# Turning the state read's exponentials on VectorE and moving the blocks by transfers inside the chip, in seven of eight batches

## The chip, the cores and the metric

The kernel runs on one core of one Trainium2 chip. A core has a matrix engine (TensorE, PE in the profile; PEld is its loading of weights, which overlaps the matrix work), VectorE (DVE), ScalarE (ACT), GpSimd (POOL), and SyncE (SP), which here only starts transfers. They run their own instruction streams and wait for each other by semaphores. SBUF is the memory on the chip that all of them use, PSUM the small memory into which TensorE writes its results.

The metric is the device time of one execution in microseconds (us). Before the change it is 656.82 us, the median of 3 runs (656.65 to 656.95).

## The reference

Two stages follow each other. The first is an attention between `x` (8 batches, 8 heads, 512 rows, 64 values) and a small `state` (32 rows per head), in both directions:

```python
scores  = scale * np.matmul(x, state.transpose(0, 1, 3, 2))    # softmax over 32 -> a
xread   = np.matmul(a, state)
scores2 = scale * np.matmul(state, x.transpose(0, 1, 3, 2))    # softmax over 512 -> a2
sread   = np.matmul(a2, x)
attn    = np.concatenate([xread, sread], axis=2)
```

The second is a feed-forward block over all 8 x (512 + 32) = 4608 tokens of 512 values, with a hidden width of 2048: `h = tokens @ w_in`, `g = h * tanh(softplus(h))` (called mish), and `g @ w_out`. The change is in `sread`, the state's read of `x`.

## The kernel before, in words

**The tiling.** Each matrix product in the feed-forward block is made of three products of a high and a low part (names ending in `h` and `l`), so each 128x512 piece of output costs three times the passes. For each batch the hidden width is walked in 8 slots (`SLOTS`) of 256. In a slot, `gemm1` multiplies the normalised attention (`ah`, `al`) with the state times `w_in` (`swh`, `swl`) into two PSUM banks `ph`; ScalarE applies mish and writes one tile `g`; VectorE makes its high part `gh` and its low part `gl`; and `gemm2`, two slots later (`LAG`), multiplies these with `w_out` (`wo`) into four PSUM banks `acc`. There is a single `g` tile, so mish of a slot waits until `gl` of the slot before has read it, and there are two `ph` banks, so `gemm1` of a slot waits until mish of the slot before has read them.

**The attention of the next batch** runs beside this. In the loop at the end of the kernel, `key` is the batch whose feed-forward slots run, and `own` is the attention of batch `key + 1`, `prev` that of batch `key`. In slot 3 (slot 4 where `key` is 1), `scores` writes the scaled scores `scs` (128 partitions: 4 head pairs x 32 state rows; two halves `kc` of 512 columns), `soft2` makes the exponentials `e2` of the state read with their sums, and `soft1` those of the other direction, which are then turned by VectorE (`at`) and split into `ah` and `al`. The state read, `sread`, is done a batch later, in slot 3 or 4 of its own batch (for batch 7 in slot 7 of batch 6).

**The step that changes.** `sread` needs `e2` with the 512 positions on the partitions. `e2_transposed` (L376) does that: for each half `kc`, four TensorE transposes of 128x128 into a PSUM bank `e2p`, then one copy by ScalarE to `e2T` in SBUF. For batches 2 to 7 it runs in slot 6 of the batch before (L865), for batch 1 in slot 2 of its own (L859), for batch 0 among the steps of the long string.

**What sets the order.** Up to the end of that string every engine issues in the written order (`InOrder`). From there on only TensorE does (`dve.on = act.on = False`); VectorE, ScalarE and the transfers are ordered by a scheduler before the kernel runs, under the written dependences. Nearly all transfers are issued by SyncE on one queue, in order, and each also waits until the one eight places ahead has landed. That queue carries the loads of `x` in two layouts (`x`, and `xq` in 32x32 blocks: 32 transfers of 32 KB per batch, in pieces of 128 bytes), the state (`sn`), and the stores of results, whose staging tiles `o` are three.

Instructions are all recorded at one helper line, L70, so this text goes by tile names.

Of the kernel before, what the change touches and what calls it, by code (L numbers as in the profile page):

```python
# [9 lines left out]
F32 = mybir.dt.float32  # L10
# [7 lines left out]
P = 128  # L18
B, H, S, NS, D = 8, 8, 512, 32, 64
DM, DF = 512, 2048  # L20
T = S + NS
NC = H // 2
NT = S // P
# [25 lines left out]
def quad(q):  # L49
    return slice(q * NS, (q + 1) * NS)  # L50
# [27 lines left out]
def state_attention_mish_kernel(ctx, tc, x, state, w_in, w_out, out):  # L78

    nc = tc.nc  # L80
    pe, dve, act, pool_e = (InOrder(tc, e) for e in (nc.tensor, nc.vector, nc.scalar, nc.gpsimd))
# [3 lines left out]
    pool = ctx.enter_context(tc.tile_pool(name="pool", bufs=2))  # L85
# [4 lines left out]
    def misc(name):  # L90
        return ps_m.tile([P, 512], F32, tag="m", name=name)
# [117 lines left out]
    def load_state(b):  # L209


        sn = pool.tile([P, H, 32], F32, tag="sn", name=f"sn_{b}", bufs=1)
        if b == 0:
            for g in range(2):
                nc.scalar.dma_start(
                    sn[:, 2 * g:2 * g + 2].rearrange("p h d -> p (h d)"),
                    state[b, 4 * g:4 * g + 4].rearrange("h n d -> (h n) d"))
            return sn
        if b == 1:
            sq[b] = pool.tile([P, H, D], F32, tag="e2T", name=f"sq_{b}")  # L220
            for q in range(4):
                nc.sync.dma_start(sq[b][quad(q)], state[b].rearrange("h n d -> n h d"))
        for q in range(4):
            nc.sync.dma_start(
                sn[q * 32:(q + 1) * 32], state[b].rearrange("h n d -> n h d")[:, :, q % 2 * 32:(q % 2 + 1) * 32])
        return sn
# [39 lines left out]
    @contextmanager  # L266
    def behind(*marks):

        with ExitStack() as st:
            for m in marks:  # L270
                st.enter_context(tc.issue_after(last[m].ins if hasattr(last[m], "ins") else last[m]))
            yield

    bds, bqs, sq = {}, {}, {}
# [8 lines left out]
    def attention(b, sn, xq=None):  # L283
        sc, e2T, srd, aT = {}, {}, {}, {}
# [70 lines left out]
        rs2, e2s = {}, {}  # L355
# [7 lines left out]
        def soft2_e(kc):  # L363
# [9 lines left out]
            dve.reciprocal(rs2[kc], sm)  # L373
            e2s[kc] = e2

        def e2_transposed(kc):  # L376
            e2 = e2s[kc]
            pt = misc(f"e2p_{b}_{kc}")
            for t in range(NT):
                pe.transpose(pt[:, t * P:(t + 1) * P], e2[:, t * P:(t + 1) * P], ident)  # L380
            yield
            e2T[kc] = pool.tile([P, NT, P], F32, tag="e2T", name=f"e2T_{b}_{kc}")
            act.copy(e2T[kc].rearrange("p t n -> p (t n)"), pt)


# [125 lines left out]
                soft2_m(kc)  # L511
                whole(soft2_e(kc))

        own.update(soft1=soft1, soft2=soft2)
        return own


# [108 lines left out]
    def gemm2(key, fcs, gh, gl, ntok, ts=None):  # L626

        if key not in accs:
            new_accs(key, ntok)
        for t in ts or range(ntok):  # L630

            for i, fc in enumerate(fcs):
                col = (i * ntok + t) * P
                sl = slice(col, col + P)
                ops = [(gh, 1), (gh, 0), (gl, 1)]
                for n, (g, w) in enumerate(ops):
                    last["PE"] = pe.matmul(
                        accs[key][t], g[:, sl], wo[fc // 2][:, fc % 2, w],
                        start=(fc == 0 and n == 0), stop=(fc == NFC - 1 and n == 2))
            if (key, fcs[-1], t) == (B - 1, NFC - 1, ntok - 1):  # L640
                for part in (slice(0, 256), slice(256, 512)):
                    o = pool.tile([P, 256], F32, tag="e2T", name=f"o_{key}_{t}_{part.start}")
                    act.copy(o, accs[key][t][:, part])
                    (nc.scalar if part.start else nc.sync).dma_start(
                        out[key * T:key * T + S, part].rearrange("(p t) e -> p t e", t=NT)[:, t, :], o)
            elif fcs[-1] == NFC - 1:
                o = pool.tile([P, DM], F32, tag="o", name=f"o_{key}_{t}", bufs=3)
                if t % 2 == 0:
                    dve.tensor_copy(o, accs[key][t])
                else:  # L650
                    act.copy(o, accs[key][t])
                if key == "s":
                    for b4 in range(4):
                        r0 = (4 * t + b4) * T + S
                        nc.sync.dma_start(out[r0:r0 + NS, :], o[b4 * NS:(b4 + 1) * NS, :])
                else:
                    to = out[key * T:key * T + S, :]

                    pieces = [(to.rearrange("(p t) e -> p t e", t=NT)[:, t], o)]
                    if key < 2:  # L660
                        to = to[t * P:(t + 1) * P].rearrange("(p i) e -> i p e", i=NT)
                        pieces = [(to[i], o[quad(i)]) for i in range(NT)]
                    for to, part in pieces:
                        last["store"] = nc.sync.dma_start(to, part)
# [117 lines left out]
    for step in """  # L782
# [13 lines left out]
        what, i = re.fullmatch(r"([a-zA-Z]+)(\d*)", step).groups()  # L796
# [20 lines left out]
    own = at1  # L817
    srds[0] = pool.tile([P, B - 1, 2, D], F32, tag="wt", name="srds", bufs=1)
    for key, j in slots:
        if key == "s":  # L820
            if j == 0:
                second((0, 1), True)
                sreads_transposed()
                second((2, 3))
            g = gemm1_s(j)
            pending.append((key, range(4 * j, 4 * j + 4), g, 2))
            if j:
                second()
            continue
        g = split_g(f"{key}_{j}", mish(key, j, gemm1(key, j, aTs[key], sw)))  # L830
        pending.append((key, (2 * j, 2 * j + 1), g, NT))

        slow = key == 1 and j < 2
        ready = slow or len(pending) > LAG
        n = pending[0][3] // 2
        if ready and not slow:
            second(range(n), True)
        if j == 0:
            prev = own
            if key + 1 < B:  # L840
                own = attention(key + 1, sn_next, xqs.pop(key + 1))
                aTs[key + 1] = own["aT"]
        more = key + 1 < B
        if key == 1 and j == 0:
            prev["soft2"]()


        beside = []
        if key == 1 and j == 1:
            beside += [sw_slice(key, 2)]  # L850
        if j == (3 if key == 1 else 1):
            beside += [sw_slice(key, 6, bank=first_bank), sw_slice(key, 4)]
        if more and j == 7:
            if 1 < key < B - 2:
                beside += [sw_slice(key + 1, 2, bank=first_bank)]
            beside += [sw_slice(key + 1, 0)]
        if key in (2, B - 1) and j == 0:
            beside += [sw_slice(key, 2)]
        if key == 1 and j == 2:  # L859
            beside += [prev["et"](k) for k in range(2)]  # L860
        if more and j == (4 if key == 1 else 3):
            beside += [own["sc"](0)]
        if j == (4 if key == 1 else 3) and key < B - 1:
            beside += [prev["sr"](k) for k in range(2)]
        if more and j == 6:  # L865
            beside += [own["et"](k) for k in range(2)]
        if key == B - 2 and j == 7:
            beside += [own["sr"](k) for k in range(2)]
        together(*beside)
        if more and j == 1:  # L870
            with behind("swl"):
                own["st"](0)
        if ready:
            second((2 * j, 2 * j + 1), j == 0) if slow else second(range(n, 2 * n))
        if more and j in (0, 2):
            with behind("swl"):
                own["x"](j)
                own["x"](j + 1)
        if more and j == (4 if key == 1 else 3):
            own["soft2"]()  # L880
        if more and j == (5 if key == 1 else 3):
            with behind("swh", "swl"):
                own["soft1"]()
        if key + 2 < B and 2 <= j < 6:

            if j == 2:
                xqs[key + 2] = new_xq(key + 2)
            with behind("store"):
                load_xq(key + 2, xqs[key + 2], range((j - 2) * H, (j - 1) * H))
        if key == 1 and j == 3:  # L890
            with behind("store"):
                xss[2] = load_x(2)
        if 1 < key < B - 1 and j == 4:
            with behind("mish"):
                xss[key + 1] = load_x(key + 1)
        if j == SLOTS - 1 and key + 2 < B:
            with behind("mish"):
                sn_next = load_state(key + 2)
# [26 lines left out]
```

## Time and profile before

| | |
|---|---|
| median of 3 runs | 656.82 us (656.65 to 656.95) |
| the profiled execution | 656.5 us, of which the span of recorded instructions is 654.7 us |
| TensorE busy | 647.8 us, 99% of the span, 4742 matrix instructions |
| VectorE busy | 341.1 us, 52% |
| ScalarE busy | 256.9 us, 39% |
| transfers | 82146 packets, 42.35 MB; the main queue takes 22.2% of the 16 transfer engines' span |

The profile is of one execution. A row of its lists names an engine, an operation and the tiles as out<-in; "x64" is a count. In a list in order of time the first column is the start and the second the length, both in us; a bracket at the end gives the idle time before the instruction and what ended it. The chain of waits is followed backwards from the last instruction, so that what it names is what set the end.

### The profile page before, as it was taken

To read this page: it belongs to the slowest core of one execution; us is meant where nothing else is said; L and a number is where in the kernel's file an instruction comes from. 1 tells how busy PE (TensorE), PEld (TensorE's weight loads), DVE (VectorE), ACT (ScalarE), POOL (GpSimd) and SP (SyncE) were. 2 spreads that over 40 slices of the span, in tenths; PEclk is the share of its full clock that TensorE was granted. 3 is DMA by queue.
4 is the path that set the end of the run, shared out by engine and by line. 5 is a ranking of instruction groups with operands and counts; after the bars stand their busy time and mean duration, and the time that the engine had idled before them with its cause. 6 is when DMAs were issued, how large, how long until landed. Compare 5 with 4: busy or idle time off the path is not lost.

```text
span 654.7 us, 11255 instructions
## 1 busy us (share of the span) xinstructions
PE 647.8 (99%) x4742; PEld 519.8 (79%) x4742; DVE 341.1 (52%) x531; ACT 256.9 (39%) x415; POOL 0.7 (0%) x6
## 2 busy tenths in 40 slices
PE   8999999999999999999999999999999999999997
PEld 6677777787778877787778887787778899878886
DVE  5999984283538245554437255544537345232222
ACT  4988943354225322542235223532235334131110
POOL 0000000000000000000000000000000000000000
PEclk9999999999999999999999999999999999999999
DMA  8986213320134003400133003400110001000001
GB/s 325 410 277 195 45 19 76 51 69 1 31 71 102 1 1 87 106 9 1 38 76 90 1 0 93 105 6 2 65 57 9 2 1 65 2 9 25 0 1 64
DMA packets 82146, 42.35 MB, mean 65 GB/s; under 512 B 63280, under 2 KB 71728, under 8 KB 82096
## 3 DMA queue, kind: packets, MB, share of 16 engines
q1 hardware_dynamic: 81664, 41.44, 22.2%
q8 instruction: 37, 0.61, 0.4%
q10 hardware_dynamic: 432, 0.20, 0.1%
q14 instruction: 13, 0.11, 0.0%
HBM read 32.70 MB, written 8.91 MB: 64 GB/s over the span
## 4 chain that ended last, share of the span: by engine, by line
PE 96%; ACT 2%; DMA 1%; SPq 0%; DVE 0%; issue 0%
PE acc L70 54%; PE ph L70 26%; PE swp L70 5%; PE ph_s L70 4%; PE acc_s L70 3%; PE srp L70 1%; PE sc L70 1%; PE e2p L70 1%; DMA wir<-in_moe_w_in_dram 1%; ACT wir L70 1%; PE scT L70 0%; SPq L128 0%; ACT L70 0%; ACT wor L70 0%; ACT swh L70 0%; ACT ah L70 0%
## 5 line engine op out<-in xcount | busy, mean ns | idle before, releaser
L70 PE MATMUL acc<-wo,gh 128*128 128x512 f32 x1024 | 319.9, 394 | 0.0
L70 PEld LDWEIGHTS acc<-wo,gh 128*128 128x128 f32 x1024 | 189.4, 188 | 46.5 <-issue 7.6
L70 PE MATMUL acc<-wo,gl 128*128 128x512 f32 x512 | 199.5, 390 | 0.0
L70 ACT ACTIVATE g<-ph 128x512 f32<-128x512 f32 x128 | 72.4, 597 | 196.6 <-DVE gl L70 166.9
L70 PEld LDWEIGHTS acc<-wo,gl 128*128 128x128 f32 x512 | 96.1, 188 | 20.5
L70 DVE CAST gh<-g 128x1024 fp32r<-128x1024 f32 (+1 forms) x61 | 41.1, 673 | 111.4 <-PE acc L70 108.6
L70 DVE TENSOR_TENSOR gl<-g,gh 128x1024 fp32r<-128x1024 f32 (+1 forms) x65 | 78.4, 1206 | 4.8 <-DVE gh L70 0.5
L70 PE MATMUL ph<-ah,swh 128*128 128x512 f32 x256 | 79.4, 392 | 0.1
L70 PE MATMUL ph<-al,swh 128*128 128x512 f32 x256 | 78.8, 390 | 0.0
L70 PE MATMUL ph<-ah,swl 128*128 128x512 f32 x256 | 78.7, 389 | 0.0
L70 DVE TENSOR_TENSOR swl<-swp,swh 128x512 fp32r<-128x512 f32 (+1 forms) x72 | 41.1, 625 | 65.0 <-ACT swh L70 65.0
L70 PEld LDWEIGHTS ph<-ah,swh 128*128 128x128 f32 x256 | 47.5, 188 | 11.3 <-ACT g L70 0.8
L70 PEld LDWEIGHTS ph<-al,swh 128*128 128x128 f32 x256 | 48.0, 188 | 10.4 <-DVE al L70 0.4
L70 PEld LDWEIGHTS ph<-ah,swl 128*128 128x128 f32 x256 | 48.1, 188 | 10.0
L70 ACT ACT_TABLE_LOAD x35 | 44.9, 1283 | 16.9 <-DVE gl L70 16.1
L70 ACT CAST swh<-swp 128x512 fp32r<-128x512 f32 (+1 forms) x72 | 34.2, 550 | 36.1 <-PE swp L70 36.1
L70 PE MATMUL swp<-w_in_sb,bd 64*32 64x256 f32 x1024 | 33.8, 381 | 0.0
L70 DVE TENSOR_REDUCE nm<-scs 128x1 f32<-128x512 f32 x16 | 10.3, 678 | 34.7 <-ACT scs L70 34.7
L70 PEld LDWEIGHTS swp<-w_in_sb,bd 64*32 64x32 f32 x1024 | 17.4, 106 | 12.7 <-issue 7.8
L70 ACT COPY o<-acc 128x512 f32<-128x512 f32 (+1 forms) x17 | 9.4, 561 | 41.7 <-PE acc L70 39.4
L70 DVE STREAM_TRANSPOSE xT<-xq 128x512 f32<-128x512 f32 x24 | 23.9, 1065 | 3.1 <-PE e2p L70 3.1
L70 DVE COPY o<-acc 128x512 f32<-128x512 f32 x16 | 10.9, 684 | 19.9 <-PE acc L70 19.9
(89 smaller groups left out, 479.1 us busy)
## 6 DMA issues: line engine op xcount, KB each, us to landing
x<-in_x_dram SPq DMA_DIRECT2D x32, 256.0 KB, 3.6
wir<-in_moe_w_in_dram SPq DMA_DIRECT2D x16, 512.0 KB, 10.0
wor<-in_moe_w_out_dram SPq DMA_DIRECT2D x16, 512.0 KB, 7.3
xq<-in_x_dram SPq DMA_DIRECT2D x192, 32.0 KB, 2.3
out_dram<-o SPq DMA_DIRECT2D x23, 256.0 KB, 2.4
out_dram<-o SPq DMA_DIRECT2D x32, 64.0 KB, 1.7
sn<-in_state_dram SPq DMA_DIRECT2D x28, 32.0 KB, 2.2
out_dram<-o_s SPq DMA_DIRECT2D x8, 64.0 KB, 1.7
```

Of the source, the lines that this page charges most:

```text
L70: made = method(*args, **kwargs)
```

## The change

For batches 1 to 7 the eight TensorE transposes and the two ScalarE copies go. In their place `e2_turned` lets VectorE turn each 128x512 half of `e2` in 32x32 blocks into a tile `u`. That leaves each block turned, but in the quarter of 32 partitions where it was. Sixteen transfers from SBUF to SBUF then take block columns from quarter `c` to quarter `q` of `e2T`; each moves 32 partitions x 8 pieces of 32 values (128 bytes), 32 KB in all. `u` has one buffer, which it shares with the scores `scs` (tag `sc`). `e2T` becomes one tile for both halves, with one buffer. The turn comes in slot 4 of the batch before (slot 6 where that is batch 1), and for batch 1 in slot 1 of its own. Batch 0 keeps its transposes. Two small tiles, `sq_1` and the last `o`, move to other tags.

```diff
         if b == 1:
-            sq[b] = pool.tile([P, H, D], F32, tag="e2T", name=f"sq_{b}")
+            sq[b] = pool.tile([P, H, D], F32, tag="o", name=f"sq_{b}", bufs=3)
...
+        def e2_turned():
+
+            both = pool.tile([P, 2 * NT, P], F32, tag="e2T", name=f"e2T_{b}", bufs=1)
+            for kc in range(2):
+                e2T[kc] = both[:, kc * NT:(kc + 1) * NT]
+            u = pool.tile([P, 2, S], F32, tag="sc", name=f"u_{b}", bufs=1)
+            for kc in range(2):
+                dve.transpose(u[:, kc], e2s[kc])
+            v = u.rearrange("i k (t q n) -> i q (k t) n", t=NT, q=4)
+            for c in range(NC):
+                for q in range(4):
+                    nc.sync.dma_start(both[quad(q), :, quad(c)], v[quad(c), q])
+
         def e2_transposed(kc):
...
-            e2T[kc] = pool.tile([P, NT, P], F32, tag="e2T", name=f"e2T_{b}_{kc}")
+            if not e2T:
+                both = pool.tile([P, 2 * NT, P], F32, tag="e2T", name=f"e2T_{b}", bufs=1)
+                e2T.update({k: both[:, k * NT:(k + 1) * NT] for k in range(2)})
...
-        if key == 1 and j == 2:
-            beside += [prev["et"](k) for k in range(2)]
+        if key == 1 and j == 1:
+            with behind("mish"):
+                prev["turn"]()
...
-        if more and j == 6:
-            beside += [own["et"](k) for k in range(2)]
...
+        if more and j == (6 if key == 1 else 4):
+            with behind("mish"):
+                own["turn"]()
```

The scheduler's order changes with it. Three places matter for the prediction. In the rows, numbers behind tile names tell buffers apart and differ between the two kernels; an `e_1` read for `u` is the exponential `e2` of batch 1.

VectorE in the first slots of batch 1, before (`at`, `al` are the turned and the low parts of batch 1's attention, `wo` and `w` the last `w_out` pieces, `swl` the low part for the first slot):

```order
L70 STREAM_TRANSPOSE at_1_1047<-e_1_1_907 128x512
L70 TENSOR_SCALAR sm_0_1161<-sm_0_1161 128x1
L70 TENSOR_SCALAR sm_1_1169<-sm_1_1169 128x1
L70 TENSOR_TENSOR wo_1045<-w_996,wo_1045 128x2x512
L70 RECIPROCAL rs_0_1164<-sm_0_1161 128x1
L70 RECIPROCAL rs_1_1172<-sm_1_1169 128x1
L70 TENSOR_TENSOR al_1050<-at_1_1047,ah_1049 128x512
L70 SCALAR_TENSOR_TENSOR w_1068<-wor_153 128x1024
```

and with the change:

```order
L70 STREAM_TRANSPOSE at_1_1046<-e_1_1_906 128x512
L70 TENSOR_SCALAR sm_0_1160<-sm_0_1160 128x1
L70 TENSOR_SCALAR sm_1_1168<-sm_1_1168 128x1
L70 STREAM_TRANSPOSE u_1223<-e_1_0_1159 128x512
L70 STREAM_TRANSPOSE u_1223<-e_1_1_1167 128x512
L70 TENSOR_TENSOR wo_1044<-w_995,wo_1044 128x2x512
L70 RECIPROCAL rs_0_1163<-sm_0_1160 128x1
L70 RECIPROCAL rs_1_1171<-sm_1_1168 128x1
L70 TENSOR_TENSOR al_1049<-at_1_1046,ah_1048 128x512
L70 SCALAR_TENSOR_TENSOR w_1067<-wor_153 128x1024
```

The two turns stand ahead of the low part of `wo`; everything behind them, up to and past `swl`, keeps its order.

VectorE in the slots where batch 4's softmaxes run (beside batch 3), from the second sum on, before:

```order
L70 TENSOR_REDUCE s_4_1_2825<-e_4_1_2823 128x16
L70 TENSOR_TENSOR e_4_0_2816<-e_4_0_2816,r_4_0_2819 128x512
L70 TENSOR_SCALAR s_4_1_2825<-s_4_1_2825 128x16
L70 STREAM_TRANSPOSE at_0_2840<-e_4_0_2816 128x512
L70 RECIPROCAL r_4_1_2826<-s_4_1_2825 128x16
L70 CAST gh_4_2875<-g_4_2872 128x1024
L70 TENSOR_TENSOR e_4_1_2823<-e_4_1_2823,r_4_1_2826 128x512
L70 TENSOR_TENSOR al_2843<-at_0_2840,ah_2842 128x512
L70 TENSOR_TENSOR gl_4_2876<-g_4_2872,gh_4_2875 128x1024
```

and with the change:

```order
L70 TENSOR_REDUCE s_4_1_2842<-e_4_1_2840 128x16
L70 TENSOR_TENSOR e_4_0_2833<-e_4_0_2833,r_4_0_2836 128x512
L70 TENSOR_SCALAR s_4_1_2842<-s_4_1_2842 128x16
L70 CAST gh_4_2892<-g_4_2889 128x1024
L70 STREAM_TRANSPOSE at_0_2857<-e_4_0_2833 128x512
L70 RECIPROCAL r_4_1_2843<-s_4_1_2842 128x16
L70 TENSOR_TENSOR gl_4_2893<-g_4_2889,gh_4_2892 128x1024
L70 TENSOR_TENSOR e_4_1_2840<-e_4_1_2840,r_4_1_2843 128x512
L70 TENSOR_TENSOR al_2860<-at_0_2857,ah_2859 128x512
```

The two turns of this batch stand some rows ahead of these (behind the reciprocals `rs`), and `gl_4` now comes ahead of two 128x512 operations that it followed. Batches 2, 3, 5, 6 and 7 show the same two moves.

SyncE's queue around batch 1's transfers, before:

```order
L224 DMA sn_1131<-in_state_dram 32x8x32 x4
L141 DMA xq_1098<-in_x_dram 32x8x32 x32
L664 DMA out_dram<-o_0_1180 32x512 x4
L664 DMA out_dram<-o_1_1192 32x512 x4
L224 DMA sn_1795<-in_state_dram 32x8x32 x3
```

and with the change:

```order
L224 DMA sn_1130<-in_state_dram 32x8x32 x4
L141 DMA xq_1097<-in_x_dram 32x8x32 x32
L387 DMA e2T_1222<-u_1223 32x8x32 x16
L680 DMA out_dram<-o_0_1179 32x512 x4
L680 DMA out_dram<-o_1_1191 32x512 x4
L224 DMA sn_1806<-in_state_dram 32x8x32 x3
```

The sixteen moves stand between the load of batch 2's `xq` and the stores of batch 0's first results. On TensorE the only rows that differ are the missing `e2p` rows of batches 1 to 7.

More of the change, by code (lines that the diff above doesn't have):

```diff
@@ L512, in soft2 @@
                 whole(soft2_e(kc))
-        own.update(soft1=soft1, soft2=soft2)
+        own.update(soft1=soft1, soft2=soft2, turn=e2_turned)
         return own
@@ L640, in gemm2 @@
             if (key, fcs[-1], t) == (B - 1, NFC - 1, ntok - 1):
+                last_o = pool.tile([P, DM], F32, tag="e2T", name=f"o_{key}_{t}", bufs=1)
                 for part in (slice(0, 256), slice(256, 512)):
-                    o = pool.tile([P, 256], F32, tag="e2T", name=f"o_{key}_{t}_{part.start}")
+                    o = last_o[:, part]
                     act.copy(o, accs[key][t][:, part])
```

## Prediction

> **What bounds the kernel now.** I read the page's busy times first, then the chain of waits, then the rows of the step that goes.
>
> ```profile
> span 654.7 us, 11255 instructions
> PE 647.8 (99%) x4742; PEld 519.8 (79%) x4742; DVE 341.1 (52%) x531; ACT 256.9 (39%) x415; POOL 0.7 (0%) x6
> PE 96%; ACT 2%; DMA 1%; SPq 0%; DVE 0%; issue 0%
> ```
>
> TensorE works for 99% of the span and makes up 96% of the chain. So TensorE time taken away is gained one to one, if what replaces it makes TensorE wait nowhere. The step that goes lies on that chain; these are the first, the third and the last of seven pieces (start, length, what), the third with the groups around it, from the chain in order of time.
>
> ```profile
> 109.24 0.88 PE e2p L70 x8
> ...
> 217.58 2.72 PE acc L70 x12
> 220.30 0.87 PE e2p L70 x8
> 221.18 2.74 PE acc L70 x12
> ...
> 511.34 0.87 PE e2p L70 x8
> ```
>
> Eight transposes hold the chain for 0.87 us, and the group of twelve products behind them takes 2.74 us where the one ahead of them took 2.72. I count 0.89 us a batch.
>
> **What is removed.** Seven batches x 0.89 us = **-6.2 us** on TensorE, and TensorE's row order differs in nothing else. ScalarE loses 14 copies, 591 ns each in the groups by shape; it is busy 39% and none of these copies is on the chain, so I count nothing.
>
> ```profile
> L70 ACT COPY e2T<-e2p 128x512 f32<-128x512 f32 x16 | 8.7, 591 | 14.8 <-PE e2p L70 12.4 <-PE srp L70 2.3
> L70 DVE STREAM_TRANSPOSE at<-e 128x512 f32<-128x512 f32 x14 | 9.9, 708 | 0.0
> L70 DVE STREAM_TRANSPOSE xT<-xq 128x512 f32<-128x512 f32 x24 | 23.9, 1065 | 3.1 <-PE e2p L70 3.1
> ```
>
> **What VectorE gets.** Two turns of 128x512 a batch. A plain one (`at`) takes 708 ns, one through a strided view (`xT`) 1065 ns. Source and target of `u` are plain rows of 512, so I take the first. Two such in a row occupy 1.22 us of the queue: the pair below starts at 270.11 and the next instruction at 271.33. Two `xT` would occupy about 1.9.
>
> ```profile
> 270.11 1.29 DVE L70 STREAM_TRANSPOSE e<-scs 128x512 f32<-128x512 f32 x2
> 271.33 0.19 DVE L70 TENSOR_SCALAR sm<-sm 128x1 f32<-128x1 f32 x2
> ```
>
> Whether that costs anything depends on who waits behind it; there are two kinds of places.
>
> **Batch 1** is the tight one. The pair goes in ahead of the row at 83.87, in a stretch where VectorE has no idle time at all until 95.05 (only that row has a bracket).
>
> ```profile
> 83.78 0.17 DVE L70 TENSOR_SCALAR sm<-sm 128x1 f32<-128x1 f32 x2
> 83.87 1.22 DVE L70 TENSOR_TENSOR wo<-w,wo 128x1024 fp32r<-128x1024 f32 x1
> ...
> 90.47 1.28 DVE L70 TENSOR_TENSOR swl<-swp,swh 128x512 fp32r<-128x512 f32 x2
> 91.66 1.99 DVE L70 STREAM_TRANSPOSE xT<-xq 128x512 f32<-128x512 f32 x2
> 95.05 0.69 DVE L70 CAST gh<-g 128x1024 fp32r<-128x1024 f32 x1 [1.40 <-ACT g L70]
> ```
>
> So `swl`, which ended at 91.75, now ends at 92.97. TensorE loads it as weights for the first slot of batch 1:
>
> ```profile
> 92.19 0.41 PEld L70 LDWEIGHTS ph<-ah,swl 128*128 128x128 f32 x2
> 86.06 0.62 PE L70 MATMUL acc<-wo,gh 128*128 128x512 f32 x2
> ```
>
> The second of these loads began at 92.41 (0.19 before its end at 92.60). Between VectorE and its waiter lie about 0.09 us (the `gl` that ends at 284.65 and the table load at 284.74, quoted below). 92.97 + 0.09 - 92.41 = **+0.65 us** of TensorE waiting. The low part of `wo` at 83.87 is late too: it now ends at 86.31, and the second product at 86.06, which begins about 86.29, needs it. That is some 0.1 us, and lies inside the 0.65, because VectorE sets the later time on its own. What comes next recovers: `gh` at 95.05 had 1.40 us of idle time ahead of it, more than the 1.22. Bounds: 0 if the pair is hidden by something I don't see, and 1.33 with turns as slow as `xT`'s.
>
> **Batches 2 to 7.** Here the pair goes in at 273.35 (batch 4, the others alike), and the chain to watch is `gl`, then ScalarE's table load, then mish `g`, then the next `gemm1`, which needs the PSUM bank.
>
> ```profile
> 273.22 0.21 DVE L70 RECIPROCAL rs<-sm 128x1 f32<-128x1 f32 x2
> 273.35 0.67 DVE L70 TENSOR_TENSOR e<-e,mx 128x512 f32<-128x512 f32 x1
> 279.59 0.69 DVE L70 TENSOR_REDUCE s<-e 128x16 f32<-128x512 f32 x1 [2.74 <-ACT e L70]
> 282.23 0.68 DVE L70 TENSOR_TENSOR e<-e,r 128x512 f32<-128x512 f32 x1
> 282.82 0.68 DVE L70 TENSOR_TENSOR al<-at,ah 128x512 fp32r<-128x512 f32 x1
> 283.43 1.22 DVE L70 TENSOR_TENSOR gl<-g,gh 128x1024 fp32r<-128x1024 f32 x1
> 284.74 1.28 ACT L70 ACT_TABLE_LOAD   x1 [2.46 <-DVE gl L70]
> 286.04 1.09 ACT L70 ACTIVATE g<-ph 128x512 f32<-128x512 f32 x2
> 287.23 0.41 PEld L70 LDWEIGHTS ph<-ah,swh 128*128 128x128 f32 x2
> ```
>
> The first half of `g` is done at 286.04 + 0.54 = 286.58, and the load that needs its bank begins at 287.23: 0.56 us to spare after 0.09 for the wait. The softmax chain shifts by 1.22, so the sum at 279.59 goes to 280.81. But the new order puts `gl` ahead of the two operations at 282.23 and 282.82, which occupied 1.20 us. So `gl` starts at 283.43 + 1.22 - 1.20 = 283.45. I count **nothing**: the cover is that 0.56 us, and without the changed order each of the six batches would lose 1.22 - 0.56 = 0.66. The two operations that now follow `gl` make `ah` and `al` for a batch that begins three slots later.
>
> **What the queue gets.** Sixteen transfers a batch. The nearest rows are the `xq` transfers: same 32 KB, same 128-byte pieces, but from memory outside the chip.
>
> ```profile
> L141 SPq DMA_DIRECT2D xq<-in_x_dram x192: 560/607/1822, 60.2 to 424.9; - x192
> DMA to landing us min/median/max: 2.0/2.3/4.6
> 60.21 23.21 SPq L141 DMA_DIRECT2D xq<-in_x_dram  x32
> 96.50 3.65 SPq L664 DMA_DIRECT2D out_dram<-o  x8
> 129.62 1.03 PE srp L70 x64
> 521.41 1.03 PE srp L70 x64
> ```
>
> At 23.21 / 32 = 0.73 us each, 16 take 11.6 us of the queue. For batch 1 they run from about 85.2 to 96.8 and have landed by 99.1; the read `srp` is at 129.62. Behind them wait the stores that issued at 96.50 and now come some 0.3 us later. The shortest way is batch 7's: `u` is made at about 493, the moves are down by 507, and the read is at 521.41. All hidden, **0 us**. While `xq` ran, TensorE was as busy as ever, so I expect no contention either.
>
> **What the wait costs TensorE.** The first four `srp` matmuls of a batch waited on 5 semaphores in all; in the listing of the new order they wait on 18, since eight transfer counters are involved.
>
> ```profile
> PEld swp L70 <- issue: 7.8, 22, 0.4
> PEld srp L70 <- issue: 3.0, 8, 0.4
> ```
>
> The start of such a group costs 7.8 / 22 = 0.355 us for `swp` and 3.0 / 8 = 0.375 for `srp`: 0.02 more, which I put to the 5 semaphores. Thirteen more are 0.05 a batch, **+0.35 us** for seven (0 at least; with 0.4, the longest of each row, in place of 0.375 it would be 0.045 x 13 / 5 x 7 = 0.8).
>
> **The sum.** -6.2 + 0.65 + 0.35 = -5.2. The span becomes 649.5, the profiled execution (656.5 before, 1.8 around its span) 651.3. The median of the runs lay 0.3 above that execution, so the forecast is 656.82 - 5.2 = **651.6 us**. The bounds give 650.6 (nothing lost) to 652.7 (1.33 and 0.8 lost).
>
> **Rivals.**
>
> *Nothing is lost:* TensorE's removal is all there is, 656.82 - 6.2 = 650.6. For it: the lost pieces are small. Against: the batch 1 stretch is full.
>
> *The turns are as slow as `xT`'s:* +1.33 at batch 1, and 1.9 - 1.20 - 0.56 = 0.14 in six batches, so 656.82 - 6.2 + 1.33 + 0.35 + 0.84 = 653.1. Against: the plain shapes of the turn.
>
> *VectorE's extra work lands on the path in every batch:* the shift is not taken up by the order, 0.66 x 6 = 4.0 more, 655.6; with slow turns (1.9 - 0.56) x 6 = 8.0 and 1.33, so 660.3. Against: 2.74 us of idle time at 279.59 is of waits, not of work, and `gl` does move ahead. The Trainium skill ("VectorE: DVE Perf Modes", Rules for kernel authors) says to transpose 128x128 on TensorE where PSUM may be the target; by that rule this rival would hold. The trace agrees that TensorE is quicker (0.89 us against 1.22 and the moves), but the rule weighs one operation alone, and here TensorE is the busy engine.
>
> *The moves are slow and hold up the queue (slower):* in batch 1 the stores of batch 0 stand behind them. The fourth result waits for the first store's tile, and TensorE for that result's bank.
>
> ```profile
> 103.83 0.59 ACT L70 COPY o<-acc 128x512 f32<-128x512 f32 x1 [1.82 <-PE acc L70]
> 111.32 0.62 PE L70 MATMUL acc<-wo,gh 128*128 128x512 f32 x2
> ```
>
> That bank is written at 111.32 at the latest, so the copy must start by 110.5, and the first four stores (1.8 us to issue, 1.7 to land) by 107.0: 16 moves may take 107.0 - 85.2 = 21.8 us, 1.36 each. From there every 0.1 us more costs 1.6. At 2.3 us each, if each waited for its landing, the loss is 15 us: 666.6. For it: a single `xq` took 1.82. Against: the median is 0.61, eight are in flight, and nothing here leaves the chip. The Trainium skill ("DMA: Bandwidth & Descriptors", Specifications) asks for at least 512 bytes a piece; the same page ("Why small descriptors are slow (HBM only)") excepts moves inside the chip. No run so far shows which holds.
>
> That the change doesn't do what it says I leave out: the order shows the `e2p` rows gone.
>
> **How the numbers follow.** Forecast 58%, nothing lost 15%, slow turns 13%, every batch 7%, slow moves 7%. Range 650.3 to 654.5: it holds the first three with 0.3 below and over 1 us above, and leaves out the last two. About 0.2% (1.3 us) is what a measurement of this kernel can tell from no change. Faster takes the first three, 86%; 655.6 is within 0.2%, so same gets 5%; the rest, 9%, is slower.
>
> **What would show it.** `e2p` x8 left, with batch 0 alone; `u<-e` near 0.7 us; a wait of PEld for `swl` or its `ph` of 0.5 to 0.8 us near 92 and no wait for `g` in later batches; `e2T` moves issued at about 0.7 us and landed before 100 in batch 1; `srp` groups starting at most 0.1 us later than before. A row of PEld waiting for `ACT g` six times, or stores of batch 0 after 100, would make me wrong.

## The result, and the profile after

The changed kernel takes 651.69 us, the median of 6 runs (651.05 to 651.87), against 656.74 us (656.59 to 657.6) for the kernel before on the same chip: a ratio of 0.992, 95% interval 0.9907 to 0.9932. The forecast was 651.6. The profiled execution took 651.86 us, its span 650.1. Which terms of the sum made that up is another matter, and two of them were wrong.

First the page of the changed kernel (span, busy times, chain of waits by engine).

```profile
span 650.1 us, 11350 instructions
PE 642.0 (99%) x4686; PEld 514.0 (79%) x4686; DVE 348.6 (54%) x545; ACT 249.5 (38%) x401; POOL 0.7 (0%) x6
PE 96%; DMA 2%; ACT 1%; DVE 0%; issue 0%; SPq 0%
```

TensorE has 56 instructions less and 5.8 us less of busy time; it is still the chain. VectorE has 14 more, 7.5 us. Next, the rows of the tiles `e2p` and `u`: the transposes that are left (durations in ns: least, median, most; then the first and last start), the moves and the turns.

```profile
L70 PE MATMUL e2p<-ident,e x8: 270/272/273, 41.9 to 45.4; 128*128 128x128 f32 x8
...
L387 SPq DMA_DIRECT2D e2T<-u x112: 586/609/1532, 85.6 to 499.5; - x112
L70 DVE STREAM_TRANSPOSE u<-e x14: 669/683/701, 84.3 to 488.4; 128x512 f32<-128x512 f32 x14
DMA to landing us min/median/max: 1.9/1.9/4.0
```

Batch 0's eight transposes are left. A turn takes 683 ns, the plain kind. A move takes 609 ns to issue, just as a load of `xq` did, and lands 1.9 us later, where `xq` took 2.3.

The tight place, batch 1, in order of time:

```profile
84.29 1.29 DVE L70 STREAM_TRANSPOSE u<-e 128x512 f32<-128x512 f32 x2
85.51 1.18 DVE L70 TENSOR_TENSOR wo<-w,wo 128x1024 fp32r<-128x1024 f32 x1
85.61 11.01 SPq L387 DMA_DIRECT2D e2T<-u  x16
86.75 0.19 PEld L70 LDWEIGHTS acc<-wo,gh 128*128 128x128 f32 x1 [0.24 <-DVE wo L70]
92.07 1.28 DVE L70 TENSOR_TENSOR swl<-swp,swh 128x512 fp32r<-128x512 f32 x2
92.81 0.19 PEld L70 LDWEIGHTS ph<-ah,swl 128*128 128x128 f32 x1
93.01 0.89 PE L70 MATMUL ph<-ah,swl 128*128 128x512 f32 x2
93.40 0.19 PEld L70 LDWEIGHTS ph<-ah,swl 128*128 128x128 f32 x1 [0.41 <-DVE swl L70]
95.96 0.69 DVE L70 CAST gh<-g 128x1024 fp32r<-128x1024 f32 x1 [0.69 <-ACT g L70]
97.40 3.65 SPq L680 DMA_DIRECT2D out_dram<-o  x8
```

The turns hold VectorE from 84.29 to 85.51, 1.22 us, and TensorE's loading waits twice: 0.24 us for `wo`, 0.41 us for `swl`. The pair of matmuls around the second wait takes 0.89 us, where such a pair takes 0.62. At `gh` the delay is gone: VectorE idles again, for 0.69 us. The last move is issued by 96.62, and the stores that stand behind the moves start at 97.40, so the moves didn't hold them up.

In batch 4, as in the other five, no weight load waits for `g` that didn't before:

```profile
271.87 1.28 DVE L70 STREAM_TRANSPOSE u<-e 128x512 f32<-128x512 f32 x2
...
279.30 0.69 DVE L70 TENSOR_REDUCE s<-e 128x16 f32<-128x512 f32 x1 [2.74 <-ACT e L70]
...
281.94 1.16 DVE L70 TENSOR_TENSOR gl<-g,gh 128x1024 fp32r<-128x1024 f32 x1
...
284.50 1.09 ACT L70 ACTIVATE g<-ph 128x512 f32<-128x512 f32 x2
...
285.87 0.41 PEld L70 LDWEIGHTS ph<-ah,swh 128*128 128x128 f32 x2
```

The sum at 279.30 keeps its 2.74 us of idle time ahead. The first half of `g` is done at 284.50 + 0.54 = 285.04, 0.83 before the load at 285.87 (before: 0.65, with the 0.09 of the wait still to come off both). The cover grew.

And the state read of batch 1. Its first matmul starts at the same time in both profiles, which makes them easy to compare; before, then after:

```profile
129.55 0.94 PEld L70 LDWEIGHTS srp<-x,e2T 128*32 128x32 f32 x64 [0.41 <-issue]
...
130.58 0.73 PE L70 MATMUL acc<-wo,gh 128*128 128x512 f32 x2
```

```profile
129.56 1.14 PEld L70 LDWEIGHTS srp<-x,e2T 128*32 128x32 f32 x64 [0.41 <-issue]
...
130.79 0.74 PE L70 MATMUL acc<-wo,gh 128*128 128x512 f32 x2
```

The idle time ahead of the group is the same 0.41 us. The group itself takes 0.20 us longer, 1.14 against 0.94 for the same 64 loads. This loss shows in no bracket and no list of waits; in the lists of the profile only the group's length and the start of the next group tell of it.

So I took the starts of all 182 groups of TensorE's work behind the long string of batch 0, in the profile of before and in each other profile, and noted where the distance between the two changes. It changes in four kinds of places, and this is the sum for the changed kernel, in us:

| place | change |
|---|---|
| up to 67 us (start-up and batch 0, where nothing is altered) | +0.48 |
| batch 1, at `wo` (0.12) and `swl` (0.30) | +0.42 |
| the seven places where `e2p` stood, 0.89 or 0.90 each | -6.27 |
| the seven state reads | +0.81 |
| end of TensorE's last group | -4.56 |

Without the first row, which turns out not to belong to the change (below), that is -5.04, against -5.05 between the medians.

### The profile page after: what moved, and what is told of

Read it like the earlier page. It is cut to its first block, busy times and chain, and to the rows that moved or that the text cites. A ratio compares the mean times of both kernels' runs of the same rounds, so it can differ in the third digit from the quotient of the medians.

```text
span 650.1 us, 11350 instructions
## 1 busy us (share of the span) xinstructions
PE 642.0 (99%) x4686; PEld 514.0 (79%) x4686; DVE 348.6 (54%) x545; ACT 249.5 (38%) x401; POOL 0.7 (0%) x6
## 4 chain that ended last, share of the span: by engine, by line
PE 96%; DMA 2%; ACT 1%; DVE 0%; issue 0%; SPq 0%
PE acc L70 55%; PE ph L70 27%; PE swp L70 5%; PE ph_s L70 4%; PE acc_s L70 3%; DMA wor<-in_moe_w_out_dram 1%; PE srp L70 1%; PE sc L70 1%; DMA x<-in_x_dram 0%; DVE s L70 0%; DVE e L70 0%; ACT L70 0%; ACT wor L70 0%; ACT ah L70 0%; ACT wir L70 0%; PE srTp L70 0%
```

## The experiments

After each run stands what it told; the table at the end has all of them in the form just shown.

**Is it batch 1's place that costs, and nothing else of VectorE's work?** The first kernel gives batch 1 its TensorE transposes back:

```diff
-        if key == 1 and j == 1:
-            with behind("mish"):
-                prev["turn"]()
+        if key == 1 and j == 2:
+            beside += [prev["et"](k) for k in range(2)]
```

> Batch 1 keeps its eight TensorE transposes in slot 2; batches 2 to 7 are turned by VectorE and moved as in the change. Theory: the 0.42 us that TensorE loses in batch 1 (0.12 waiting for wo, 0.30 for swl) comes from the two turns in VectorE's full stretch, so no wait for wo or swl near 86 to 93 us is left, the 0.20 us at batch 1's state read goes too, and 0.89 us of transposes comes back: 0.3 us slower than the change, about 652.0. Rival (the waits come from the later start of this execution, which lay 0.46 us behind at 63 us): both waits stay, 0.9 us slower.

651.98 us (651.6 to 652.18), ratio 0.9925 [0.991, 0.994]. Neither wait of batch 1 is there, the read of batch 1 loses nothing, six removals stay. Against the changed kernel this loses the 0.89 of batch 1 and wins 0.42 there and about 0.2 at the read: the turn of batch 1 was worth its stall.

The second keeps the turn but lets the scheduler put it behind `swl`:

```diff
-            with behind("mish"):
+            with behind("mish", "swl"):
                 prev["turn"]()
```

> As the change, but batch 1's two turns wait for the low part swl of the first slot, so that on VectorE they come behind swl and xT. Theory: the 0.42 us of waiting for wo and swl is gone and nothing replaces it, since 1.40 us of VectorE's idle time followed there before the change: 0.4 us faster than the change, 651.3. Its moves start about 8 us later and share the queue with the stores of batch 0. Rival (VectorE's work counts wherever it stands): the wait reappears at the next gemm1 or at mish of slot 2, time as the change's 651.7.

651.09 us (650.51 to 651.2), ratio 0.991 [0.9895, 0.9925]. The rows of its batch 1:

```profile
93.29 1.26 DVE L70 STREAM_TRANSPOSE u<-e 128x512 f32<-128x512 f32 x2
94.58 2.60 SPq L387 DMA_DIRECT2D e2T<-u  x4
94.89 0.69 DVE L70 CAST gh<-g 128x1024 fp32r<-128x1024 f32 x1 [0.34 <-ACT g L70]
97.27 3.84 SPq L680 DMA_DIRECT2D out_dram<-o  x8
101.15 7.78 SPq L387 DMA_DIRECT2D e2T<-u  x12
```

The turn now stands in the idle time ahead of `gh`, of which 0.34 us is left, and no load waits for `wo` or `swl`. The moves are partly behind the stores and still long done by 129. The 0.42 us is a price of the place.

**Does the amount of VectorE's work count in batches 2 to 7?** Each pair of turns is done twice:

```diff
-            for kc in range(2):
+            for kc in (0, 1, 0, 1):
                 dve.transpose(u[:, kc], e2s[kc])
```

> The changed kernel, with each batch's pair of turns done twice on VectorE (the second pair writes the same values over the first); moves and read as they are. Theory (the place counts, not the amount: VectorE has cover in batches 2 to 7 and none in batch 1): in batch 1 swl comes another 1.22 us late, so the wait of TensorE for it grows from 0.30 to about 1.5; in batches 2 to 7 nothing, because the scheduler is free to put the second pair where there is room and 0.56 us of cover and about 2 us of idle time ahead of the second sum stand there; together +1.2, about 652.9 us. Rival (VectorE's time counts in each batch): +1.2 and 6 x (1.22 - 0.56) = 4.0 more, about 657, with six new waits of weight loads for g.

652.35 us (652.01 to 652.8), ratio 0.994 [0.9927, 0.9954], far from the rival's 657. That is 0.76 above the changed kernel on that chip, where the theory had 1.2; the profiles give 0.97, because the state reads lost less here (the table at the end). Batch 1 loses 1.64 in place of 0.42, the 1.22 of the second pair:

```profile
93.61 0.19 PEld L70 LDWEIGHTS ph<-ah,swl 128*128 128x128 f32 x1 [1.24 <-DVE swl L70]
94.21 0.19 PEld L70 LDWEIGHTS ph<-ah,swl 128*128 128x128 f32 x1 [0.41 <-DVE swl L70]
```

and batch 4, again as the other five, nothing:

```profile
276.17 1.30 DVE L70 STREAM_TRANSPOSE u<-e 128x512 f32<-128x512 f32 x2
...
280.09 0.69 DVE L70 TENSOR_REDUCE s<-e 128x16 f32<-128x512 f32 x1 [2.05 <-ACT e L70]
...
284.17 1.09 ACT L70 ACTIVATE g<-ph 128x512 f32<-128x512 f32 x2
...
286.59 0.41 PEld L70 LDWEIGHTS ph<-ah,swh 128*128 128x128 f32 x2
```

The second pair went into the idle time ahead of the second sum (2.05 left of 2.74), and `g` is done even earlier before the load that needs its bank.

**What do the moves cost, and what the waits at the read?** One kernel leaves out turns and moves, the other only the reading of what they make:

```diff
 def e2_turned():
-    both = pool.tile([P, 2 * NT, P], F32, tag="e2T", name=f"e2T_{b}", bufs=1)
     for kc in range(2):
-        e2T[kc] = both[:, kc * NT:(kc + 1) * NT]
+        e2T[kc] = w_in_sb[:, kc, :S].rearrange("p (t n) -> p t n", t=NT)
+    return
```

> Leaves out the turns and the moves of batches 1 to 7 altogether: the state read of these batches takes part of the weights w_in in place of the turned exponentials, so its result is not the reference's. What is left is the removal of the transposes alone. Theory: 0.89 us a batch is all that TensorE gains, and the change gives back 0.42 us (turns in batch 1) and 0.8 us (waits at the state reads): 1.2 us faster than the change, 650.5, and no more. Rival (the moves or turns also slow the rest, by contention): more than 1.6 us faster, with other groups of products shorter.

650.49 us (650.16 to 650.84), ratio 0.9901 [0.9885, 0.9918]. Of the sum only the -6.27 is left: 0.02 at the reads and 0.02 in batch 1. This is what the rival "nothing is lost" had forecast for the change, 650.6.

```diff
 def e2_turned():
     both = pool.tile([P, 2 * NT, P], F32, tag="e2T", name=f"e2T_{b}", bufs=1)
     for kc in range(2):
-        e2T[kc] = both[:, kc * NT:(kc + 1) * NT]
+        e2T[kc] = w_in_sb[:, kc, :S].rearrange("p (t n) -> p t n", t=NT)
```

> Turns and moves run as in the change, but the state read of batches 1 to 7 takes part of w_in in place of what was moved, so its first matmuls wait on 5 semaphores as before the change, and not on 18 (the result is not the reference's). Theory (the waits themselves cost TensorE's time): the 0.20 us of batch 1's state read and the 0.04 to 0.12 us of the others go, 0.8 us faster than the change, 650.9; the 0.42 us in batch 1 stays. Rival (moves and reads collide, or rows written by transfers are read more slowly): the state reads stay as long as with the change.

651.58 us, its runs wide apart (649.93 to 652.52), ratio 0.9917 [0.99, 0.9933], so the profile has to speak (the profiled execution took 652.06 us, but its span is only 649.1, against the 650.1 of the changed kernel's). Batch 1 loses 0.49, as with the change; the seven reads lose 0.02. The read of batch 1:

```profile
129.35 0.94 PEld L70 LDWEIGHTS srp<-x,w_in_sb 128*32 128x32 f32 x64 [0.41 <-issue]
```

It has its 0.94 us back, with all 112 moves running. So the 0.81 us is not contention by the moves; it comes with reading what they made.

**Is there room in the queue?** Each move is issued twice:

```diff
-            for c in range(NC):
+            for c in (*range(NC), *range(NC)):
```

> The changed kernel, with the 16 moves of each batch issued twice (same source, same target, the same 8 counters). Theory (hidden in the queue): 32 moves at 0.69 us are 22 us of the queue; the first use of what they make is 33 us behind in batch 1 and about 4 us behind the last landing in batch 7, so +0 (within 0.5 us), and the srp groups lose as little as with 16 (0.04 to 0.20 us each, the counters being the same). In batch 1 the stores of batch 0 stand behind 20 of them and come about 3 us later than with the 16, at 100 instead of 97, against a bound of 107. Rival (the moves collide with other transfers, or the queue has no room): slower by over 1 us, with a wait of TensorE for a transfer at srp, or for a bank of acc behind a late store near 110.

651.68 us (650.98 to 652.46), ratio 0.993 [0.9917, 0.9944]; the changed kernel had 651.59 on that chip. Its moves, its stores in batch 1, and the queue at batch 7:

```profile
L387 SPq DMA_DIRECT2D e2T<-u x224: 586/609/1492, 85.5 to 509.9; - x112
99.48 3.84 SPq L680 DMA_DIRECT2D out_dram<-o  x8
488.92 21.61 SPq L387 DMA_DIRECT2D e2T<-u  x32
```

The stores start at 99.48 in place of 97.40, and nobody waits for them; batch 7's last move is issued by 510.5, and the read comes at 516.5. The queue could carry twice as many moves. The prediction's refuting sign, stores of batch 0 after 100, was all but reached here without any loss: by its own bound of 107 the sign was set too early.

**What is it in the read that costs?** With the change, the first four matmuls of each read wait on 18 semaphores (four or more each), before on 5. The transfers use eight counters in turn (in the trace 14 of the change's 112 moves stand on each), so the last eight moves stand on the same counters as the first eight, and waiting for the last covers the first. The order of the four heads decides how many waits are left:

```diff
             for t in range(NT):
-                for h4 in range(4):
+                for h4 in (3, 2, 1, 0):
```

> The changed kernel, with the four head products of each position block of the state read issued in the order 3, 2, 1, 0 in place of 0, 1, 2, 3. The last transfers stand on the same counters as the first ones, so waiting for the last covers the first: the read of each batch waits on 9 or 10 semaphores, at two matmuls, in place of 18, at four. So far the seven state reads lost 0.5 to 0.8 us in all with 18 semaphores (six profiles) and 0.02 to 0.04 with 5 (two profiles). Theory (the price goes by the number of semaphores): 4 to 5 above the five, of 13, leaves 0.15 to 0.3 us in all, so 0.4 us less than the changed kernel. Rival (the price is for reading what transfers have just written, or for the first wait on a transfer counter at all): 0.5 to 0.8 us as before.

650.38 us (649.93 to 650.8), ratio 0.9901 [0.9887, 0.9915]. The reads lose 0.03 us in all, less even than the theory's 0.15 to 0.3, so a price that goes evenly by the number of semaphores is out, and the rival too. The group of batch 1:

```profile
128.92 0.94 PEld L70 LDWEIGHTS srp<-x,e2T 128*32 128x32 f32 x64 [0.41 <-issue]
```

Four or five extra semaphores cost nothing, thirteen 0.5 to 0.8 us. One run stands between them, at three matmuls. Its expectation counts 14 or 15 semaphores; the instructions in its trace hold 13 or 15:

```diff
-                for h4 in range(4):
+                for h4 in (1, 3, 2, 0):
```

> The changed kernel, with the head products of the state read in the order 1, 3, 2, 0: 14 or 15 semaphores, at three matmuls. With 18 at four the seven reads lost 0.5 to 0.8 us, with 9 or 10 at two 0.01 and 0.02, so the price is not even per semaphore from 5 on. Theory A (up to about 10 are free, and what lies above costs evenly): 4 of the last 8 are left, 0.25 to 0.4 us in all. Theory B (what costs is the fourth wait of its kind, or the last few): 0 to 0.1 us. Theory C (what costs is waiting on a counter twice, which this order still does for four of eight): 0.25 us or more, with the third matmul free to start. A and C look alike here; B differs. The time by A: 0.2 to 0.4 us under the changed kernel.

650.67 us (650.29 to 650.82), ratio 0.9911 [0.9894, 0.9929], and 0.02 us at the reads. The time is the one that theory B gives, and A and C are out; waiting on a counter twice is free as such. But B's reason, that the fourth waiting matmul costs, doesn't hold either, as the waits themselves show.

The number of instructions on the page tells that waits are instructions of their own: nothing was altered but that order, and there are 11350 in the changed kernel, with 18 semaphores, and these with the orders 1, 3, 2, 0 and 3, 2, 1, 0:

```profile
span 648.9 us, 11332 instructions
```

```profile
span 648.7 us, 11318 instructions
```

The Trainium skill ("Perfetto Trace Analysis", Identifying Dependency Chains) says that an instruction which waits on several engines may have further instructions put ahead of it that hold the other waits; the counts agree.

The lists of the profile leave these instructions out, but the trace records each of them (`EVENT_SEMAPHORE`, 51 ns, with one or two semaphores). In TensorE's stream the first of a read begins 0.79 to 0.93 us before the read's first load, while the matmuls ahead are still running, and most follow each other at 0.11 to 0.13 us. The table has all 98 reads, seven in each of the fourteen profiles; times are in us from the read's first load, and the last load tells how long the group is:

| waiting instructions in a read | reads | the last one ends at | the last load starts at |
|---|---|---|---|
| 1 (before; no moves, or moves unread; batch 1 with transposes) | 22 | -0.87 to -0.82 | 0.83 |
| 4 or 5 (order 3, 2, 1, 0) | 14 | -0.53 to -0.37 | 0.83 |
| 6 or 7 (order 1, 3, 2, 0) | 7 | -0.23 to -0.14 | 0.83 |
| 8 (17 semaphores, four matmuls) | 7 | 0.00 to 0.04 | 0.84 to 0.87 |
| 9 (18 semaphores, four matmuls) | 48 | 0.04 to 0.20 | 0.88 to 1.03 |

In each of the 55 reads with eight or nine, the group is longer by the time at which its last wait ends, to within 0.01 us. So the price is neither one for each semaphore nor one for the fourth waiting matmul: up to seven waiting instructions fit into the time that TensorE's stream is ahead, and what sticks out beyond it delays the loads. Six of the seven reads with eight, which wait at four matmuls too, lose only 0.01 us; three of these are in the kernel with the turns done twice, which is why its reads lost less. In the change, the loads of the seven reads are late by 0.63 us in all, and the rest of the 0.81 shows in the groups that follow. Batch 1's read loses most because 0.28 us, and not 0.11 to 0.13, lie between the starts of its seventh and its eighth wait; what makes that pause, and what sets the lead of 0.9 us, the trace doesn't tell.

**Both repairs together**, and the measures for them:

```diff
-            with behind("mish"):
+            with behind("mish", "swl"):
                 prev["turn"]()
...
-                for h4 in range(4):
+                for h4 in (3, 2, 1, 0):
```

> Batch 1's turn placed as in e2_late_turn, and the state read's products in the order of e11_last_first: both repairs at once, meant as the best version. Theory: no stall in batch 1, 0.15 to 0.3 us at the seven state reads, so 0.3 to 0.5 us under e2_late_turn and 0.8 under the changed kernel, about 650.5, close to the 650.5 of the kernel without turns and moves. Rival (the waits cost the same in any order): as e2_late_turn.

650.59 us (649.52 to 652.36), ratio 0.9909 [0.9893, 0.9926]. Its profile has no loss left: 0.01 in batch 1 and 0.02 at the reads.

```profile
span 648.5 us, 11320 instructions
PE 640.7 (99%) x4686; PEld 513.3 (79%) x4686; DVE 348.6 (54%) x545; ACT 249.6 (38%) x401; POOL 0.7 (0%) x6
```

It beats the kernel before and, by the profile, the change by 1.2 us (-6.24 against -5.04). Its median and that of the version with the order of heads alone (650.38) can't be told apart; their runs overlap, and by the profiles 0.44 us lies between them.

> The kernel of e2_late_turn a third time, as the measure for the two others of this call: about 651, with 0.5 to 0.75 us at the seven state reads.

650.92 us (650.65 to 651.76), ratio 0.9912 [0.9897, 0.9926], with 0.69 at the reads, on the chip of the two kernels before it.

> The kernel of e2_late_turn once more, beside the changed kernel on the same chip. Theory: it lacks the 0.42 us of batch 1 and nothing else differs, so it is 0.4 us under the changed kernel (0.3 to 0.7), about 651.2. Rival (the 0.6 us between the two earlier runs are scatter): no difference beyond 0.2 us.

650.84 us (650.44 to 651.66), ratio 0.992 [0.9906, 0.9933].

> The changed kernel once more, unedited, as the measure for the other kernels of this call. If the start-up's +0.46 us in its first profile was scatter between executions, the offset at 63 us in this profile differs from it by up to 0.8 us; if the change caused it, it is +0.4 to +0.5 again. The 0.42 us in batch 1 and the small losses at the srp groups should be there again within 0.1 us each.

651.59 us (651.2 to 652.76), ratio 0.9931 [0.9918, 0.9943]: 0.75 above the late turn on the same chip, where the profiles give 0.45. Its start-up stands at -0.15, where the first profile of the same kernel had +0.48: not a cost of the change. The three profiles of the late turn (-0.18, -0.48, +0.15) come from three chips, and four kernels on one chip, alike up to there, stray from -0.18 to +0.15; how much is of the chip and how much of the execution the runs don't separate. Batch 1 loses 0.45 again, the reads 0.74.

All profiles against that of before, in us; "sum" leaves the start-up out; the last column is the difference between the kernel's median and that of the kernel before on the same chip:

| kernel | start-up | batch 1 | `e2p` gone | reads | sum | medians |
|---|---|---|---|---|---|---|
| the change | +0.48 | +0.42 | -6.27 | +0.81 | -5.04 | -5.05 |
| the change again | -0.15 | +0.45 | -6.27 | +0.74 | -5.08 | -4.66 |
| batch 1 on TensorE | +0.50 | 0.00 | -5.38 | +0.63 | -4.75 | -4.92 |
| late turn | -0.18 | +0.01 | -6.27 | +0.53 | -5.73 | -5.81 |
| late turn, second | -0.48 | 0.00 | -6.27 | +0.74 | -5.53 | -5.41 |
| late turn, third | +0.15 | 0.00 | -6.27 | +0.69 | -5.58 | -5.95 |
| turns twice | +0.07 | +1.64 | -6.27 | +0.52 | -4.11 | -3.90 |
| moves twice | +0.36 | +0.47 | -6.27 | +0.71 | -5.09 | -4.57 |
| no turns, no moves | -0.35 | +0.02 | -6.27 | +0.02 | -6.23 | -6.41 |
| moves unread | +0.20 | +0.49 | -6.27 | +0.02 | -5.76 | -5.32 |
| last heads first | -0.18 | +0.44 | -6.27 | +0.03 | -5.80 | -6.49 |
| three waiting matmuls | +0.04 | +0.48 | -6.27 | +0.02 | -5.77 | -5.66 |
| late turn, last first | +0.14 | +0.01 | -6.27 | +0.02 | -6.24 | -6.28 |

The columns of the terms repeat within 0.1 us (the reads within 0.3) from kernel to kernel; the medians stray by up to 0.7 from the sum.

## Why the prediction was right, and where it wasn't

**What is removed (-6.2): right.** -6.27, seven times 0.89 or 0.90, in every profile in which all seven are gone. TensorE was the chain, and nothing else held the place of its time.

**The turns (1.22 us a pair, by the plain kind): right.** 1.22 from 84.29 to 85.51, 683 ns each. The rival "slow turns" falls with that.

**Batch 1 (+0.65): the right mechanism, the size too large by 0.23.** With that profile's start-up of 0.48 taken off, `swl` ended at 92.87 and not at 92.97, and the load began 0.05 later and not 0.09 (93.35 to 93.40), so at 92.92: it was late by 0.51, not by 0.65. And of those 0.51 the matmuls lost 0.42: the idle time of the loading (0.24 and 0.41 in the brackets) isn't TensorE's loss one to one (0.12 and 0.30 in the starts of the groups). The step that failed is "92.97 + 0.09 - 92.41", which took a load's lateness for TensorE's loss. That it is the place that costs was shown by the late turn (0.01) and by the turns done twice (1.64).

**Batches 2 to 7 (0, with 0.56 of cover): right.** No load waits for `g` that didn't before. In batch 4 the second sum comes 1.07 us later in relation to TensorE's load (1.22 forecast), and `gl`, moved ahead of two operations as the changed order said, 0.13 earlier, so the cover grew. The bound "0.66 each without the changed order" was the wrong way to ask: with the turns doubled, the scheduler placed them anew in idle time, and the six batches lost nothing. The rival "every batch" is out. The rule of the Trainium skill ("VectorE: DVE Perf Modes", Rules for kernel authors), to transpose 128x128 on TensorE where PSUM may be the target, would have been the slower choice here: VectorE's way takes longer (1.22 us a batch and the moves, against 0.89) and wins, as it is off the chain.

**The queue (0): right.** 0.69 us a move in batch 1 (11.01 / 16) against 0.73; twice as many moves cost nothing. The stores came 0.9 later and not 0.3, of which TensorE's own lateness in that profile is 0.9 (0.48 + 0.42), so in relation to it they are not late at all. The "slow moves", due from 1.36 us each, are far off. The Trainium skill ("DMA: Bandwidth & Descriptors", Why small descriptors are slow (HBM only)) excepts moves inside the chip from the penalty for small pieces. The trace agrees in direction: with pieces of 128 bytes they cost what the loads from outside cost to issue, 609 ns against 607, and land sooner, 1.9 us against 2.3. No run here moves the same data in larger pieces, so what the smallness itself costs is not shown.

**What the wait costs TensorE (+0.35, 0 to 0.8): wrong in mechanism.** It measured 0.74 and 0.81 in the two profiles of the change, at and just over the upper end. The step that failed is "thirteen more are 0.05 a batch", which put the longer start of `srp` to its 5 semaphores and multiplied. The start of a read, its 0.41 us of idle time, never changed. The loss lies inside the group, and it isn't counted per semaphore: it is the time by which the last waiting instruction ends after the first load, nothing with up to seven such instructions and 0.05 to 0.20 us a read with the nine of the change. The sign given for it, "srp groups starting at most 0.1 later", looked at the wrong end of the group.

**The sum (-5.2): right by two errors of opposite sign,** -0.23 and +0.39 to +0.46, which leave -5.04 and -5.08. That the total came out so close is luck. The start-up's -0.48 to +0.50 and the medians' own spread are as large as either error, so the median alone would have confirmed every term.

## What to carry to other kernels

Where one engine is the chain, work moved off it is worth its full time there even if it takes longer elsewhere, and what it costs is a matter of the place in the other engine's queue: look for the stretch without idle time ahead of something the chain loads, and put the work behind it. If one large product is fed by many small transfers, count how many waiting instructions stand ahead of the product, and issue first the matmul that waits for the last transfers on each counter; here that order alone was worth 0.7 to 0.8 us by the profiles. And make the ledger place by place: a sum that agrees with the median can hide errors that cancel.

## What the runs showed of the hardware that I hadn't expected

Waits at the head of a group of matmuls are instructions in TensorE's stream, 0.11 to 0.13 us apart as a rule, and they begin 0.8 to 0.9 us before the group. Up to seven of them cost nothing; with eight or nine the group is longer by as much as the last one ends after its first load, 0.01 to 0.20 us. The cost appears in no list of waits, only in the length of the group (1.14 us against 0.94) and in the trace's records of the waits themselves. And the start-up of one and the same kernel differs by 0.6 us between two profiles (+0.48, -0.15), which is more than batch 1's whole loss.
